# Recurrent attention and a squared-ReLU layer on one core: asking for the next pair's inputs a few product rows later, with the opening and the first groups put in another order

## The chip, the core and the metric

The kernel runs on one NeuronCore of a Trainium2 chip. The metric is the device time of one execution in microseconds (us), as the median of several runs. Besides the timed runs there is one profiled execution, from which every row and line below comes. The engines are called as in the profile: PE (TensorE's matrix products), PEld (its weight loads), DVE (VectorE), ACT (ScalarE), POOL (GpSimd) and SP (SyncE, which here only issues transfers).

## What is computed

```python
# attention: B=4 batches, H=8 heads, S=768 steps, D=48 per head
for t in range(S):
    state = alpha[:, :, t, :, None] * state + einsum('bhd,bhe->bhde', k[:, :, t], v[:, :, t])
    y[:, :, t] = einsum('bhd,bhde->bhe', q[:, :, t], state)
x = y.transpose(0, 2, 1, 3).reshape(B * S, H * D)      # 3072 tokens x 384
# feed-forward layer
h = maximum(x @ w_in, 0.0)                             # 384 -> 2048
out = (h * h) @ w_out                                  # 2048 -> 384
```

All of q, k, v and alpha arrive in 32-bit floats. The two weight matrices arrive in 64-bit floats.

## The kernel before

**Blocks, pairs and groups.** The sequence is cut into chunks of 128 steps, which gives 24 blocks (six chunks by four batches). Attention treats blocks two at a time, called a pair here. Four blocks make a group of 512 tokens, and the feed-forward layer runs once for each of the six groups, numbered 0 to 5. While the layer of one group runs on PE, attention for the next group's blocks is woven into it.

**One block of attention.** `load` (L119) brings alpha, q, k and v, each 192 KB, in a transfer of their own. `ln` (L258, ACT) takes the logarithm of alpha, `cs` (L280, and L283/L284 for later blocks, PE) sums it up along the steps, `eb` and `ei` (L291, L295, ACT) make the factor and its inverse, `mq` and `mk` (L299, DVE) scale q and k by them. `kT`/`qT` (L351) and later `turn` (L567) transpose on PE, and `kc`/`qc` (L365, later L575) copy the result out of PSUM. `sc` (L410) and `kv` (L438) form scores and state sums on PE, `am` (L421), `us` (L451) and `st` (L467, L468) mask and advance the state on DVE. `ga` and `gb` hold these for the two blocks of the pair `n0` and also the products y (L390) of the pair before; `ev` (L605, ACT or DVE) copies y into x, the layer's input.

**The layer.** In group 0 it uses plain 32-bit products: `ffn_in` (L908) with its relu and square on ACT (L914, L917). Later groups split each operand into parts (`b`, `l`, `d` of weights and `a`, `l`, `d` of activations) and use three fast products instead: L715 for the first matrix, L798 for the second. The parts of the weights are made once during groups 0 and 1 (`prepare`: L647 on ACT, then L642 twice on DVE), stored to DRAM by L652, and fetched again by L683 when a buffer is free.

**The weights' conversion.** A piece of 64-bit weights is loaded by L136 or L140 and turned into 32 bits in three steps, `convert_first` (L163, L167 on DVE), `convert_middle` (L177, L180 on ACT) and `convert_second` (L188, L192, L195 on DVE).

**What sets the order.** Each engine executes its own instructions in the order in which the Python code emits them. Three devices set that order.

- The opening is written out by hand, as a string of steps (`AT['first']`), and `AT['pre']` gives its first loads. In that string `ha0` is the first half of hidden tile 0 (the 256 tokens of blocks 0 and 1) and `hb1` the second half of tile 1; `zeros` is a set of three products on zeros whose result nobody reads.
- After it, `weave` goes through a list of units of PE work, each with a cost in product rows (a row is about six L715 products), and emits every event whose time, in rows, has come.
- `attention` makes the events of a pair from two tables of times (`PLAN`, `EARLY`) and numbers of `AT`: `g0`, `g1` and `g` say when each pair starts in group 0, group 1 and the groups after, `sc0` stretches the table in group 0, `ga` and `gb` are the rows at which those two stand.

In `attention`, the loads of the next pair's inputs are events too. They hang on the step that frees their buffer: alpha on `cs`, q on `turn`, keys on `ga` and `gb`, v on `gb`:

```python
        def loads(at, *which):
            out.extend((at, load, (m, x)) for m, x in which if m < NBLK)
```

SP issues all transfers in the order of emission: the inputs, the stores of parts (L652), their fetches (L683), a small row of factors through DRAM (`bl`, L317, and `br`, L327) and the outputs (L922). At most eight transfers are in flight, as transfer i waits for transfer i-8 to land. An issue that waits holds up everything behind it on SP.

## Time and profile before

| | |
|---|---|
| timed runs | 525.36, 529.82 and 524.78 us; median 525.36 us |
| the profiled execution | 526.78 us, of which its span is 525.0 us |
| PE busy | 511.3 us, 97% of the span |
| DVE busy | 362.9 us, 69% |
| ACT busy | 305.2 us, 58% |
| transfers | 102.35 MB, mean 195 GB/s |
| granted TensorE clock | 1.00 in every slice |

The page divides the span into 40 slices of 13.1 us and gives the busy share of each engine. A matmul's end is modelled, so a busy PE only says that matmuls followed each other without a hole. Its waits (who waited for whom) tell what ended each hole; "issue" there means that the engine waited for nothing that the profile shows.

### The profile page before, as it was taken

The numbers are of one execution on the slowest core, as the hardware profiler recorded it, in microseconds if no ns is written. First come the engines' busy times: TensorE is split into PE (matmuls) and PEld (weight loads), VectorE is DVE, ScalarE is ACT, GpSimd is POOL, SyncE is SP. The second block draws the span as 40 slices with busy tenths as digits, with TensorE's granted clock in tenths as the row PEclk, the third lists the DMA queues.
The fourth block names the chain that finished last, engine by engine and source line by source line (L and its number), as shares of the span: only waits on it lengthen the run. The fifth ranks groups of instructions, "written<-read, shape, count | busy, mean of one in ns | idle before, by whom it ended". The sixth has DMA issues, their size and how long they took to land.

```text
span 525.0 us, 13021 instructions
## 1 busy us (share of the span) xinstructions
PE 511.3 (97%) x5346; PEld 421.9 (80%) x5346; DVE 362.9 (69%) x627; ACT 305.2 (58%) x650; POOL 5.3 (1%) x29
## 2 busy tenths in 40 slices
PE   8879999999999999999999999999999999999997
PEld 6665455669888669887899987889987899988997
DVE  3677979989879859766596566686464486463861
ACT  5658896575779645475963166953265763164620
POOL 4000000000000000000000000000000000000000
PEclk9999999999999999999999999999999999999999
DMA  9998877555589665998995787855683444699201
GB/s 189 228 248 169 238 162 180 112 153 227 182 221 218 173 192 157 286 305 201 203 263 167 236 234 196 228 162 167 208 282 126 159 151 139 212 373 308 82 2 60
DMA packets 139323, 102.35 MB, mean 195 GB/s; under 512 B 109808, under 2 KB 112896, under 8 KB 139264
## 3 DMA queue, kind: packets, MB, share of 16 engines
q1 hardware_dynamic: 139264, 101.52, 68.6%
q8 instruction: 42, 0.69, 0.5%
q14 instruction: 17, 0.14, 0.1%
HBM read 84.17 MB, written 17.33 MB: 193 GB/s over the span
## 4 chain that ended last, share of the span: by engine, by line
PE 92%; SPq 3%; issue 1%; DMA 1%; ACT 1%; DVE 1%; DVEq 0%; POOLq 0%
PE o L798 41%; PE h L715 31%; PE h L908 7%; PE y L390 4%; SPq L119 3%; PE sckv L410 2%; PE T L567 2%; PE sckv L438 2%; DMA raw<-in_moe_w_in_dram 1%; PE cs L283 1%; PE cs L284 1%; PE cs L280 1%; SPq L136 0%; ACT hid L917 0%; PE lastT L334 0%
## 5 line engine op out<-in xcount | busy, mean ns | idle before, releaser
L715 PE MATMUL h<-xa,wb 128*128 128x512 f32 x240 | 68.8, 395 | 0.0
L715 PE MATMUL h<-xl,wl 128*128 128x512 f32 x240 | 67.8, 391 | 0.9 <-issue 0.9
L715 PE MATMUL h<-xd,wd 128*128 128x512 f32 x240 | 66.7, 393 | 0.1
L605 ACT COPY x<-y 32x256 f32<-32x256 f32 (+3 forms) x134 | 47.9, 365 | 23.2 <-PE y L390 21.0
L637 DVE TENSOR_TENSOR hid<-h,hid 128x512 f32<-128x512 f32 x40 | 27.6, 689 | 46.9 <-PE h L715 46.7
L732 ACT ACTIVATE h<-h 128x512 f32<-128x512 f32 x40 | 23.3, 582 | 62.2 <-PE h L715 62.2
L798 PE MATMUL o<-wb,ha 128*128 128x384 f32 x160 | 54.4, 340 | 1.3 <-issue 1.3
L715 PEld LDWEIGHTS h<-xl,wl 128*128 128x128 f32 x240 | 45.0, 188 | 11.0 <-issue 1.1
L798 PE MATMUL o<-wd,hd 128*128 128x384 f32 x304 | 53.8, 334 | 0.0
L798 PE MATMUL o<-w_out,hid 128*128 128x384 f32 x160 | 53.7, 490 | 0.0
L798 PE MATMUL o<-wl,hl 128*128 128x384 f32 x160 | 53.5, 335 | 0.0
L798 PEld LDWEIGHTS o<-wd,hd 128*128 128x128 f32 x304 | 52.7, 188 | 0.2
L715 PEld LDWEIGHTS h<-xd,wd 128*128 128x128 f32 x240 | 44.5, 188 | 9.7 <-issue 0.5
L715 PEld LDWEIGHTS h<-xa,wb 128*128 128x128 f32 x240 | 44.3, 188 | 9.1
L798 PE MATMUL o<-wb,hx 128*128 128x384 f32 x144 | 48.7, 338 | 0.0
L798 PE MATMUL o<-wl,hx 128*128 128x384 f32 x144 | 48.1, 334 | 0.0
L908 PE MATMUL h<-x,w_in 128*128 128x512 f32 (+1 forms) x120 | 43.3, 510 | 2.9 <-issue 2.0
L798 PEld LDWEIGHTS o<-w_out,hid 128*128 128x128 f32 x160 | 29.9, 190 | 19.9 <-ACT w_out L180 0.2
L730 ACT ACTIVATE hid<-h 128x512 f32<-128x512 f32 x40 | 24.2, 606 | 29.3 <-PE h L715 29.2
L690 ACT ACTIVATE ha<-hid 128x512 fp32r<-128x512 f32 x40 | 25.4, 637 | 25.6 <-DVE hx L642 17.2
L908 PEld LDWEIGHTS h<-x,w_in 128*128 128x128 f32 x120 | 22.3, 190 | 20.4 <-issue 16.9
L642 DVE SCALAR_TENSOR_TENSOR hl<-ha,hid 128x512 fp32r<-128x512 f32 x40 | 27.5, 686 | 12.2 <-ACT ha L690 12.2
(114 smaller groups left out, 869.4 us busy)
## 6 DMA issues: line engine op xcount, KB each, us to landing
wd<-do SPq DMA_DIRECT2D x36, 384.0 KB, 4.9
wl<-lo SPq DMA_DIRECT2D x34, 384.0 KB, 4.4
wl<-li SPq DMA_DIRECT2D x32, 384.0 KB, 4.2
wd<-di SPq DMA_DIRECT2D x32, 384.0 KB, 3.5
raw<-in_moe_w_in_dram SPq DMA_DIRECT2D x8, 768.0 KB
raw<-in_moe_w_out_dram SPq DMA_DIRECT2D x8, 768.0 KB, 4.8
v_in<-in_v_dram SPq DMA_DIRECT2D x24, 192.0 KB, 4.3
out_dram<-osb SPq DMA_DIRECT2D x24, 192.0 KB, 2.4
```

Of the source, the lines that this page charges most:

```text
L119: nc.sync.dma_start(out=t[:, :, 0:D] if x in "qk" else t.rearrange("a (h d) -> a h d", h=H), in_=srcs[x][b, :, c * C : (c + 1) * C, :].rea ...
L390: ins = nc.tensor.matmul(out=ys[e][64 * half : 64 * half + D + G * e, m % 2, p // 2, t], lhsT=lhsT, rhs=rhs, start=(half, e) not in seen, ...
L410: nc.tensor.matmul(out=ps[e][HALF[h], 0, p, :], lhsT=ks[rows, p, HALF[h]], rhs=qs[rows, p, HALF[h]], start=True, stop=True, skip_group_che ...
L605: copy(out=x[kk][to : to + m, t : t + 2], in_=blk[n]["y"][e][r : r + m, :, p // 2],)
L637: nc.vector.tensor_tensor(out=o, in0=x, in1=z, op=op)
L642: nc.vector.scalar_tensor_tensor(out=o, in0=x, scalar=c, in1=y, op0=ALU.mult, op1=op)
L690: nc.scalar.activation(out=a, in_=x, func=AF.Copy, scale=NEAR * E)
L715: nc.tensor.matmul(out=acc["h", j], lhsT=here[w, "i", p][:, kk, jj * 128 : (jj + 1) * 128], rhs=x_parts[x][:, kk], start=start and kk == 0 ...
L730: nc.scalar.activation(out=hid[j], in_=x, func=AF.Copy, scale=E)
L732: nc.scalar.activation(out=x, in_=x, func=AF.Copy, scale=1.0 + E)
L798: nc.tensor.matmul(out=acc[t][:, 0:DM], lhsT=lhs[:, t * C : (t + 1) * C], rhs=rhs, start=start, stop=stop, skip_group_check=True,)
L908: nc.tensor.matmul(out=ps, lhsT=w[:, kk, c0 : c0 + 128], rhs=xT[g][kk][:, cols], start=(kk == 0), stop=(kk == KM - 1),)
```

## The change

The calls of `loads` get delays of their own, from a new tuple `later`, in product rows. It holds where the table is not stretched (`scale == 1`: groups 1 to 4), and is zero in group 0.

```diff
     def attention(t, n0, after, scale=1, begun=True, whole_at=None, turn_at=None):
         out = []
+        later = AT["later"] if scale == 1 else (0,) * 7
...
                 if f == "ga":
-                    loads(w, (n0 + 3, "k"))
+                    loads(w + later[0], (n0 + 3, "k"))
                 elif f == "gb":
-                    loads(w, (n0 + 2, "v"), (n0 + 3, "v"), (n0 + 4, "k"))
+                    for i, m, x in ((1, n0 + 2, "v"), (2, n0 + 3, "v"), (3, n0 + 4, "k")):
+                        loads(w + later[i], (m, x))
...
                 elif f == "turn":
                     out.append((w, turn, (n0,)))
-                    loads(w, (n0 + 2, "q"), (n0 + 3, "q"))
+                    loads(w + later[4], (n0 + 2, "q"))
+                    loads(w + later[5], (n0 + 3, "q"))
...
                     if f[:-1] == "cs":
-                        loads(w, (n + 2, "a"))
+                        loads(w + later[6], (n + 2, "a"))
```

The entries of `AT` that change (the others are as before):

```diff
+'later': (0, 2, 2, 0, 1, 3, 2)
-'evs': 0.65   'w_first': (44.75, 40.75, 51.5)   'w_in_at': 2.375   'w_in_by': 3.4   'room1': 22   'xs': 0.2
+'evs': 0.7    'w_first': (42.75, 40.5, 48.5)    'w_in_at': 2.5     'w_in_by': 2.6   'room1': 23   'xs': 0.0
-'g0': ((0.75, 4, False, True, 25.5), (21.25, 6, True, True), (28.25, 8, True, False))   'sc0': (2.15, 2.35, 2.35)
+'g0': ((0.5, 4, False, True, 25.5), (21.75, 6, True, True), (28.0, 8, True, False))     'sc0': (2.35, 2.35, 2.35)
-'g1': ((5.75, 8, False, 15.5), (15.25, 10, True), (34.5, 12, True))   'g': ((1.575, 6, True), (15.5, 8, True))
+'g1': ((5.5, 8, False, 16.25), (15.0, 10, True), (34.5, 12, True))    'g': ((2.075, 6, True), (14.0, 8, True))
-'g1x': 50.0   'h0': 17   'h1': 0    'evs0': 0.1   'o0': (46.5, 47.25)    'o2': (19.75, 27.0, 32.75, 34.0, 42.0, 41.75)
+'g1x': 52.5   'h0': 16   'h1': -1   'evs0': 0.5   'o0': (48.25, 47.25)   'o2': (16.75, 28.5, 30.5, 34.75, 41.25, 42.5)
-'str1': 24.5   'ga': 9.5    'gb': 12.75   'cv0': 1.125   'pre': '0a 1a 0q 0k 1k 1q'   'cp': ()
+'str1': 24.0   'ga': 10.0   'gb': 12.25   'cv0': 0.875   'pre': '0a 0q 1a 0k 1k 1q'   'cp': ('q0', 'k1', 'k0')
-'evd': (... (2, 0, 2), (2, 1, 1), (2, 1, 2), (2, 1, 3))
+'evd': (... (2, 0, 2), (2, 1, 0), (2, 1, 1), (2, 1, 2), (2, 1, 3))
-'first': '... load2k lt1 sc1 kv1 first0 load2q load3a load2v am1 ... load3v load3k ep02 kT2 weights1 kc2 zeros2 load3q
-          second0 lt0 sc2 eb3 kv2 ei3 ep03 zeros3 first1 weights2 middle1 ha0 mq3 mk3 qT3 load4k kT3 qc3 kc3 am2 load4q
-          ha1 second1 sc3 lt2 lt3 st0 kv3 am3 us2 ha2 us3 load4a first2 ya2 yb2 weights3 ep20 ep21 ha3 weights4
-          ep22 ep23 middle2 st3 hb1 load4v second2 weights5 weights6 st2 hb2 st1 hb3 hb0'
+'first': '... load2k kT1 us0 kc1 lt1 sc1 kv1 first0 load3a ... load2q load3q ei2 ya0 ln3 yb0 load3v ... weights1 load2v
+          ep02 kT2 load3k cs3 kc2 weights2 eb3 lt0 sc2 second0 ei3 zeros3 ep03 mq3 kv2 first1 middle1 ha0 qT3 mk3 load4k
+          kT3 kc3 am2 qc3 load4a ha1 second1 sc3 lt3 st0 kv3 am3 us2 lt2 us3 ha2 first2 ya2 st1 yb2 ep20 load4v ep21 ha3
+          load4q ep22 ep23 middle2 st3 weights6 second2 weights4 hb1 st2 hb2 hb0 hb3 weights5 weights3'
```

`cp` names the copies of the opening's transposes that DVE makes instead of ACT (three), `evd` those of y (one more). One of the three `zeros` sets is left out. Whichever number stands behind `weights`, the next piece in order is loaded.

More of the change, by code (lines that the diff above doesn't have):

```diff
@@ L18 @@
 GB = 4
-AT = {'evs': 0.65, 'lead': 4, 'post': 3, 'w_first': (44.75, 40.75, 51.5), 'wstep': 1.8, 'w_in_at': 2.375, 'w_in_by': 3.4, 'room1': 22, 'room': 24, 's0': 4, 'ahead': 6, 'late': 2, 'xs': 0.2, 'g0': ((0.75, 4, False, True, 25.5), (21.25, 6, True, True), (28.25, 8, True, False)), 'sc0': (2.15, 2.35, 2.35), 'g1': ((5.75, 8, False, 15.5), (15.25, 10, True), (34.5, 12, True)), 'g': ((1.575, 6, True), (15.5, 8, True)), 'g1x': 50.0, 'gx': 46.75, 'g0x': 56.25, 'k0': 2, 'h0': 17, 'k1': 4, 'h1': 0, 'h1by': 2, 'evs0': 0.1, 'tp': 'ADMD', 'tp1': 'ADAD', 'split': 8, 'o0': (46.5, 47.25), 'o1': (), 'o2': (19.75, 27.0, 32.75, 34.0, 42.0, 41.75), 'str1': 24.5, 'ga': 9.5, 'gb': 12.75, 'cv0': 1.125, 'pre': '0a 1a 0q 0k 1k 1q', 'cp': (), 'evd': ((0, 0, 0), (0, 1, 0), (0, 1, 2), (2, 0, 2), (2, 1, 1), (2, 1, 2), (2, 1, 3)), 'first': 'ln0 warm0 ln1 cs0 zeros3 ei0 mk0 eb0 mq0 kT0 cs1 qT0 kc0 eb1 load0v load2a qc0 mq1 sc0 ei1 ln2 qT1 mk1 weights0 qc1 kv0 am0 load1v us0 kT1 kc1 load2k lt1 sc1 kv1 first0 load2q load3a load2v am1 middle0 cs2 eb2 us1 ei2 ya0 yb0 mk2 ln3 mq2 qT2 qc2 cs3 ep00 ep01 load3v load3k ep02 kT2 weights1 kc2 zeros2 load3q second0 lt0 sc2 eb3 kv2 ei3 ep03 zeros3 first1 weights2 middle1 ha0 mq3 mk3 qT3 load4k kT3 qc3 kc3 am2 load4q ha1 second1 sc3 lt2 lt3 st0 kv3 am3 us2 ha2 us3 load4a first2 ya2 yb2 weights3 ep20 ep21 ha3 weights4 ep22 ep23 middle2 st3 hb1 load4v second2 weights5 weights6 st2 hb2 st1 hb3 hb0'}
@@ new lines @@
+AT = {'later': (0, 2, 2, 0, 1, 3, 2), 'evs': 0.7, 'lead': 4, 'post': 3, 'w_first': (42.75, 40.5, 48.5), 'wstep': 1.8, 'w_in_at': 2.5, 'w_in_by': 2.6, 'room1': 23, 'room': 24, 's0': 4, 'ahead': 6, 'late': 2, 'xs': 0.0, 'g0': ((0.5, 4, False, True, 25.5), (21.75, 6, True, True), (28.0, 8, True, False)), 'sc0': (2.35, 2.35, 2.35), 'g1': ((5.5, 8, False, 16.25), (15.0, 10, True), (34.5, 12, True)), 'g': ((2.075, 6, True), (14.0, 8, True)), 'g1x': 52.5, 'gx': 46.75, 'g0x': 56.25, 'k0': 2, 'h0': 16, 'k1': 4, 'h1': -1, 'h1by': 2, 'evs0': 0.5, 'tp': 'ADMD', 'tp1': 'ADAD', 'split': 8, 'o0': (48.25, 47.25), 'o1': (), 'o2': (16.75, 28.5, 30.5, 34.75, 41.25, 42.5), 'str1': 24.0, 'ga': 10.0, 'gb': 12.25, 'cv0': 0.875, 'pre': '0a 0q 1a 0k 1k 1q', 'cp': ('q0', 'k1', 'k0'), 'evd': ((0, 0, 0), (0, 1, 0), (0, 1, 2), (2, 0, 2), (2, 1, 0), (2, 1, 1), (2, 1, 2), (2, 1, 3)), 'first': 'ln0 ln1 warm0 cs0 ei0 zeros3 mk0 eb0 kT0 cs1 mq0 qT0 kc0 eb1 load0v load2a qc0 sc0 ei1 mq1 ln2 weights0 qT1 mk1 qc1 kv0 am0 load1v load2k kT1 us0 kc1 lt1 sc1 kv1 first0 load3a middle0 am1 us1 cs2 eb2 load2q load3q ei2 ya0 ln3 yb0 load3v mq2 qT2 mk2 ep00 ep01 qc2 weights1 load2v ep02 kT2 load3k cs3 kc2 weights2 eb3 lt0 sc2 second0 ei3 zeros3 ep03 mq3 kv2 first1 middle1 ha0 qT3 mk3 load4k kT3 kc3 am2 qc3 load4a ha1 second1 sc3 lt3 st0 kv3 am3 us2 lt2 us3 ha2 first2 ya2 st1 yb2 ep20 load4v ep21 ha3 load4q ep22 ep23 middle2 st3 weights6 second2 weights4 hb1 st2 hb2 hb0 hb3 weights5 weights3'}
```

## The prediction

> **What bounds the kernel.** I read the busy shares and slices first, then the chain that ended last, then who waited for whom on PE, then the timelines at the long waits.

> ```profile
> PE 511.3 (97%) x5346; PEld 421.9 (80%) x5346; DVE 362.9 (69%) x627; ACT 305.2 (58%) x650; POOL 5.3 (1%) x29
> PE   8879999999999999999999999999999999999997
> DMA  9998877555589665998995787855683444699201
> PE 92%; SPq 3%; issue 1%; DMA 1%; ACT 1%; DVE 1%; DVEq 0%; POOLq 0%
> ```

> PE is the bound: 511.3 of 525.0 us, 92% of the last chain, and only its first slices and the tail are not full. The transfers are nearly saturated only in the first 40 us. An order of events can save only what PE loses in holes: 525.0 - 511.3 = 13.7 us, less the tail of 3.5 us and the first loads. PE's waits, longest first:

> ```profile
> PE h L908 <- issue: 2.0, 1, 2.0
> PE y L390 <- issue: 1.7, 3, 0.7
> PE o L798 <- issue: 1.3, 1, 1.3
> PE h L715 <- issue: 0.9, 1, 0.9
> PE h L908 <- ACT x L605: 0.8, 1, 0.8
> PE sckv L438 <- DMA v_in<-in_v_dram: 0.5, 1, 0.5
> ```

> (Columns: us in total, times, the longest.) The waits for another engine or a transfer all lie in the opening. The largest have no partner: "issue". In PE's compiled program (a plain 32-bit product is four instructions, a fast one or a transposition two, a wait one) these holes stand at instructions 450, 1218, 5570, 7362, 8130 and 9155: always whole multiples of 256 apart, to one. The DMA queue for instructions shows what that is, a quiet stretch ahead of two holes and then one packet (end of one view, then of the other):

> ```profile
> q8 instruction: 1, 0.02, 2.3%
> ...
> q8 instruction: 1, 0.02, 2.6%
> ```

> The first is from 35.5 to 38.3 us, the second from 238.5 to 241.3 us; 30.5 to 35.5 and 235.2 to 238.5 us show none. Over the span the queue has 42 packets for 0.69 MB. So PE's program comes in packets of about 16 KB, 256 instructions, and PE stands still when the next isn't there. Comparing the packets' landings with the instruction that PE was at, a packet is asked for about 300 instructions ahead, queues behind the transfers in flight (0.1 to 8.5 us) and is usable some 1.4 us after its arrival. A stretch of 256 quick instructions (4 to 6 us, small attention products) gives it too little time.

> The opening's large hole and what it delays, PE then ACT:

> ```profile
> 34.84 1.35 PE L908 MATMUL h<-x,w_in 128*128 128x256 f32 x5
> 38.23 1.24 PE L908 MATMUL h<-x,w_in 128*128 128x256 f32 x5 [2.04 <-issue]
> 40.30 7.16 PE L908 MATMUL h<-x,w_in 128*128 128x256 f32 x26 [0.84 <-ACT x L605]
> ...
> 38.64 0.38 ACT L914 ACTIVATE r<-h 128x256 f32<-128x256 f32 x1 [1.76 <-PE h L908]
> 39.49 0.75 ACT L605 COPY x<-y 32x256 f32<-32x256 f32 x2
> ```

> The last product of `ha3` is the first one after the boundary and waits 2.04 us. ACT's relu (L914) and square of `ha3` come ahead of the last two copies of x (L605), so x ends at 40.24 us and `hb1` waits for it until 40.30.

> **The change, part by part.**

> *The opening's order.* One `zeros` set, three plain products of 12 instructions in all, is gone, and steps change places. By the compiled order the boundary at 1218 now falls on the fifth product of `hb1`; `ha3` is at 1197 to 1208. So neither `ha3`, its relu nor the copies of x are held by the packet. Against it, v of block 2 is asked for behind v of 3, and `kv2` waits for it about 0.37 us longer. The packet for the boundary is asked for some 0.35 us later than before (30.9 for 30.5 us), so I put it usable at 38.6 us. Work behind it can start there and not at 40.30: -1.7 us. The bounds: nothing (the packet comes 1.7 us later still, as behind the transfers of one more weight piece) and -2.1 us (x ends at 38.2). The missing `zeros` products cost nothing: they (six passes of about 0.22 us) stand where PE waits for v of block 2 anyway; without that wait they would be a gain of 1.3 us.

> *The loads later.* They stand in groups 1 to 4 only. A row is six products of 0.227 us (144 L715 products take 32.68 us), 1.36 us, so a load goes back by 1.4 to 4.1 us. From issue to first use, before: the tightest alpha pair (blocks 10, 11) lands at 145.1 and is used at 150.7 us, 5.6 us; k of 11 has 5.1 us (its own delay is 0), k of 17 7.4, v of 10 10.8, alpha of 16 10.5, q of 10 11.9, the rest at least 14. Alpha of 10 goes back 2.7 us, and behind one more store of parts on SP, leaving about 2. No wait is left on PE: cost 0. If this cover were gone, a pair's alpha 2 us late would hold PE for up to 2 us a pair. On SP the stores, fetches and outputs that stood behind these loads now go first; they get no later. [...]

> *The groups' events.* They move the boundaries in time, and so the holes. I compared PE's nominal time for the 256 instructions before each boundary in both programs, and the margin of before (negative: a hole). At instruction 4034 it goes from 5.85 to 4.61 us (margin 1.5 to 0.26); at 5570 4.99 to 4.33, less one load that no longer goes ahead of the packet (the hole stays at 0.95); at 6338 6.02 to 4.72 (2.0 to 0.7); at 7362 4.32 to 5.41 (a hole of 0.7 goes); at 7618 6.07 to 4.76 (a hole of 1.3 appears); at 8130 3.16 to 4.08 (1.27 to 0.35); at 9154 4.95 to 6.10 (0.37 goes). The sum of the holes is 3.15 us before and 2.55 after: -0.6 us. The bounds: all gone, -3.15; every one as at 1218, 2.04 us at seven boundaries, +11.1.

> *Group 0's end.* The second part of piece 6 of w_out now stands behind that of piece 7 on DVE, whose work there fills 11.7 to 11.9 of every 12.5 us. Its part is ready at 118.1 us by DVE's nominal time, and PE needs it at 118.07 to 118.25. I take +0.3 us, bounds 0 and +1. In group 1 weight parts come ahead of `mk` and `mq` by one DVE operation of 0.95 us; the thinnest margin of transposed q and k was 0.14 to 0.6 us, in the second pair. Bounds 0 and +0.8; I take 0, as that pair's start moves earlier too (15.25 to 15.0 rows). The further copies on DVE in the opening lie beside PE's wait for loads.

> **Sum.** -1.7 + 0.3 - 0.6 = -2.0 us against the profiled execution: 526.78 - 2.0 = 524.8 us. That execution is 1.42 us above the median of the runs; the median should follow: 525.36 - 2.0 = 523.4 us.

> **The rivals.**

> *A. The opening's hole only moves.* The packet comes when the transfers in flight let it, and the reordered loads put `load4v` and two weight pieces closer to it. Then the hole, 2 us, stays on the path and the rest balances: 525.4 us. For it: a hole of 2.04 us at the same boundary, in a stretch with transfers at 9 tenths. Against it: x no longer depends on it. [...]

> *B. Slower: the later loads stand in front of PE's packets.* In groups 1 to 4 the loads now leave near the small products whose stretch of 256 is shortest. A load of 192 KB takes 1.1 us to land behind another (0.9 to 1.2 us between landings in the opening). With one more ahead of each of the seven packets, the margins above give holes of 0.84, 2.05, 0.4, 0.93, 2.4, 1.45 and 0.53, sum 8.6 us: 6.05 more, 529.5 us. With two it is 16.3 us and 537 us. I put it at 531. It decides from 0.3 us of delay a packet on, the first margins. For it: the packet at 241 us waited about 3 us behind fetches and loads. Against it: the same packets have such company before, and spread loads can also clear the way.

> *C. All packets come in time.* Holes after the opening vanish (-3.15), the opening gives -2.1, group 0 nothing: 525.36 - 5.25 = 520.1 us, 520.0 rounded down. For it: four of the seven stretches get longer or lose a load. Against it: 7618 and 4034 get shorter.

> *D. The delays do nothing.* It is contained in the sum, at zero.

> **How the numbers follow.** Forecast 0.40, A 0.12, B 0.24, C 0.24. One per cent, 5.25 us, is about what a measurement of this kernel tells from no change. Faster by over that needs 520.1 or less: most of C, 0.19, and 0.03 of the forecast's edge, 0.22. Slower needs 530.6: 0.21 of B and 0.03 from delays of a thin pair, 0.24. The rest, 0.54, is within. The range goes from 517.5, C with the `zeros` gain of 1.3 and 1.2 us of PE elsewhere, to 531.5, just over B; the forecast's own range is 521.5 to 525.5.

> **What would show it.** Right: no hole over 1 us at `ha3`, x copied by 38.3 us and `hb1` going by 38.7; no wait of PE for `a_in`, `q_in` or `v_in` after 45 us; holes called "issue" at 5570 and 7618, none at 7362. Wrong: PE waiting for DVE or ACT in groups 0 to 3, for loads in groups 1 to 4, or "issue" holes above 5 us together.

## The result, and the profile after

The changed kernel takes 524.86 us, the kernel before 526.92 us, as medians of 20 runs each; the ratio is 0.9962 (95% interval 0.9944 to 0.9981), 1.0 to 3.0 us less. Three runs of the kernel before, of 847 to 1300 us, are left out of the ratio, and its median without them is 525.97 us. The forecast was 2.0 us less, a median of 523.4 us, and within 1%. The profiled execution of after took 524.59 us, its span 522.8 us against 525.0 us.

The page of after, busy time, slices and chain as shown of before:

```profile
PE 511.1 (98%) x5340; PEld 421.1 (81%) x5340; DVE 365.5 (70%) x632; ACT 304.1 (58%) x645; POOL 5.3 (1%) x29
PE   8799999999999999999999999999999999999997
PE 92%; DVE 2%; ACT 2%; SPq 1%; DMA 1%; issue 1%; POOLq 0%; DVEq 0%
```

PE is still the bound, its slices full from the third to the tail, and does six passes less, the set of zeros (a pass is one matmul of the profile; a plain 32-bit product is two). The lines of its waits in after that matter here (us in total, times, the longest):

```profile
PE sckv L410 <- ACT ks L365: 1.7, 1, 1.7
PE sckv L410 <- DVE ks L365: 0.8, 1, 0.8
PE h L908 <- DVE x L605: 0.8, 1, 0.8
PE sckv L410 <- DVE qs L365: 0.8, 1, 0.8
PE h L715 <- ACT x L605: 0.8, 2, 0.4
PE h L715 <- issue: 0.5, 1, 0.5
PE y L390 <- issue: 0.2, 1, 0.2
```

The holes called issue are down from 5.9 to 0.7 us. The opening's hole of 2.0 us and those at 318, 345 and 399 us are gone; at 241 us 0.5 is left of 0.9. In their place stand waits for copies of q and k in the opening, and two of 0.4 us for copies of x, at 248 and 329 us, within the layers of groups 2 and 3. The end of the opening, PE and then ACT of after:

```profile
34.51 1.50 PE L390 MATMUL y<-am,v_in 64*48 64x64 f32 x64
35.94 2.07 PE L908 MATMUL h<-x,w_in 128*128 128x256 f32 x8
38.80 7.94 PE L908 MATMUL h<-x,w_in 128*128 128x256 f32 x28 [0.80 <-DVE x L605]
```

```profile
37.81 0.38 ACT L914 ACTIVATE r<-h 128x256 f32<-128x256 f32 x1
38.78 0.75 ACT L605 COPY x<-y 32x256 f32<-32x256 f32 x2
```

Hidden tile 0's last product isn't held any more, and `hb1` goes on at 38.80 instead of 40.30 us. But there are two passes more to do from there (28 for 26), and the last products y, at 33.41 us before, came 1.1 us later.

For a comparison at equal work I gave every product its mean duration by kind from the profile of before, holes left out, and cut each trace where 449.5, 300, 270, 200 and 100 us of such work were left. Each row is one profiled execution, in us, up to the start of PE's last product; the kernels below the second row are the experiments.

| kernel | opening, to 449.5 left | 449.5 to 300 | 300 to 270 (holds 241 us) | 270 to 200 | 200 to 100 (holds 318, 345, 399 us) | rest |
|---|---|---|---|---|---|---|
| before | 60.17 | 153.50 | 32.30 | 70.77 | 105.86 | 98.54 |
| after | 59.46 | 153.58 | 31.95 | 71.83 | 103.69 | 98.45 |
| later_only | 58.95 | 154.38 | 32.01 | 70.77 | 107.92 | 98.54 |
| opening_only | 60.87 | 153.55 | 32.32 | 70.77 | 108.01 | 98.54 |
| no_later | 60.68 | 153.55 | 32.50 | 71.88 | 103.69 | 98.45 |
| groups_only | 58.52 | 154.10 | 34.47 | 71.55 | 103.69 | 98.44 |
| after_z12 | 61.08 | 153.67 | 32.51 | 71.38 | 103.69 | 98.44 |
| groups_nz | 58.25 | 153.56 | 31.09 | 72.11 | 103.69 | 98.44 |
| before_p96 | 61.93 | 153.54 | 34.01 | 72.31 | 102.83 | 98.54 |
| before_p48 | 63.59 | 153.56 | 35.93 | 75.50 | 102.83 | 98.54 |

Between before and after: opening -0.7, the stretch with 241 us -0.35, the next +1.1 (the first of the two waits for x, at 249 us, and a hole of 0.2 at 265 us), the stretch with 318, 345 and 399 us -2.2. Together -2.2 us.

The openings of the table can't be compared as they stand, for the granted clock differs. The profiles of opening_only and no_later show it at 0.50 for 3.4 us, from 24.8 and from 23.6 us on, while PE works without a pause. In windows of 2 us of opening_only (the clock stands behind the number of matmuls):

```profile
24.00:26.00 2.00, 2.00 (x37) 0.71 0.66 139
26.00:28.00 2.00, 2.00 (x35) 0.50 1.12 351
```

Half of that time, 1.6 to 1.7 us, is lost, so I put both openings at about 59.2 us at full clock, an estimate. After has such a stretch from 16.1 to 19.5 us, ahead of a wait of 1.7 us that takes it up; groups_nz has one from 15.8 to 19.2 us, ahead of a wait of 1.2 us; before, later_only, groups_only and after_z12 have none in the opening.

### The profile page after: what moved, and what is told of

Same layout as the page of the kernel before. It is cut to its first block, busy times and chain, and to the rows that moved or that the text cites. A ratio compares the mean times of both kernels' runs of the same rounds, so it can differ in the third digit from the quotient of the medians.

```text
span 522.8 us, 13015 instructions
## 1 busy us (share of the span) xinstructions
PE 511.1 (98%) x5340; PEld 421.1 (81%) x5340; DVE 365.5 (70%) x632; ACT 304.1 (58%) x645; POOL 5.3 (1%) x29
## 4 chain that ended last, share of the span: by engine, by line
PE 92%; DVE 2%; ACT 2%; SPq 1%; DMA 1%; issue 1%; POOLq 0%; DVEq 0%
PE o L798 40%; PE h L715 30%; PE h L908 8%; PE y L390 5%; PE sckv L410 2%; PE T L567 2%; PE sckv L438 2%; ACT x L605 1%; SPq L119 1%; DMA v_in<-in_v_dram 1%; PE cs L280 1%; DVE x L605 1%; DVE osb L637 0%; PE cs L283 0%; PE cs L284 0%
## 5 line engine op out<-in xcount | busy, mean ns | idle before, releaser
L715 PE MATMUL h<-xd,wd 128*128 128x512 f32 x240 | 68.5, 398 | 0.8 <-issue 0.5
L715 PE MATMUL h<-xa,wb 128*128 128x512 f32 x240 | 68.5, 394 | 0.8 <-ACT x L605 0.8
L715 PE MATMUL h<-xl,wl 128*128 128x512 f32 x240 | 67.7, 390 | 0.0
L605 ACT COPY x<-y 64x256 f32<-64x256 f32 (+3 forms) x132 | 47.0, 365 | 26.9 <-PE y L390 20.5
L798 PE MATMUL o<-wb,ha 128*128 128x384 f32 x160 | 54.4, 340 | 0.0
L798 PE MATMUL o<-w_out,hid 128*128 128x384 f32 x160 | 53.7, 490 | 0.0
L798 PE MATMUL o<-wd,hd 128*128 128x384 f32 x304 | 53.7, 334 | 0.0
L798 PE MATMUL o<-wl,hl 128*128 128x384 f32 x160 | 53.6, 335 | 0.0
L715 PEld LDWEIGHTS h<-xa,wb 128*128 128x128 f32 x240 | 44.5, 188 | 10.7 <-ACT x L605 1.7
L715 PEld LDWEIGHTS h<-xl,wl 128*128 128x128 f32 x240 | 45.1, 188 | 9.7
L798 PEld LDWEIGHTS o<-wd,hd 128*128 128x128 f32 x304 | 52.8, 188 | 0.0
L715 PEld LDWEIGHTS h<-xd,wd 128*128 128x128 f32 x240 | 43.9, 188 | 10.6 <-issue 1.6
L798 PE MATMUL o<-wb,hx 128*128 128x384 f32 x144 | 48.4, 336 | 0.0
L798 PE MATMUL o<-wl,hx 128*128 128x384 f32 x144 | 48.2, 334 | 0.0
L798 PEld LDWEIGHTS o<-w_out,hid 128*128 128x128 f32 x160 | 29.9, 190 | 19.7
L908 PE MATMUL h<-x,w_in 128*128 128x512 f32 (+1 forms) x120 | 43.7, 514 | 0.9 <-DVE x L605 0.8
L908 PEld LDWEIGHTS h<-x,w_in 128*128 128x128 f32 x120 | 22.1, 190 | 18.4 <-issue 14.3
L690 ACT ACTIVATE ha<-hid 128x512 fp32r<-128x512 f32 x40 | 25.4, 638 | 19.2 <-PE o L798 12.1
L637 DVE TENSOR_TENSOR osb<-o,osb 128x384 f32<-128x384 f32 x24 | 12.9, 556 | 28.2 <-PE o L798 27.0
```

The lines of the kernel that those rows point to most:

```text
L605: copy(out=x[kk][to : to + m, t : t + 2], in_=blk[n]["y"][e][r : r + m, :, p // 2],)
L637: nc.vector.tensor_tensor(out=o, in0=x, in1=z, op=op)
L690: nc.scalar.activation(out=a, in_=x, func=AF.Copy, scale=NEAR * E)
L715: nc.tensor.matmul(out=acc["h", j], lhsT=here[w, "i", p][:, kk, jj * 128 : (jj + 1) * 128], rhs=x_parts[x][:, kk], start=start and kk == 0 ...
L798: nc.tensor.matmul(out=acc[t][:, 0:DM], lhsT=lhs[:, t * C : (t + 1) * C], rhs=rhs, start=start, stop=stop, skip_group_check=True,)
L908: nc.tensor.matmul(out=ps, lhsT=w[:, kk, c0 : c0 + 128], rhs=xT[g][kk][:, cols], start=(kk == 0), stop=(kk == KM - 1),)
```

## The experiments

The theory, P: behind the opening the time hangs on where the boundaries of PE's 256-instruction packets fall, and the delays of the loads do nothing. The places bear out the first half: counting PE's passes, weight loads and waits, all 37 holes called issue in the fourteen profiles stand within one instruction of 450 plus a multiple of 256, and in before and in after the queue for instructions moves 42 packets, 0.69 MB, 16 KB each. What the holes cost is for the experiments. The first four kernels take the change apart.

**The delays alone (later_only).** The kernel before with `'later': (0, 2, 2, 0, 1, 3, 2)` and nothing else.

> The kernel before with nothing but the delays of the loads in groups 1 to 4 (`later`); PE's program is the same as before. Theory P (after the opening, the time hangs on where PE's packets of 256 instructions end, and the loads cost and bring nothing): within 0.5 us of before, with holes called issue again near 241, 318, 345 and 399 us, 2.5 to 3.5 us together. Rival L (the spread loads clear the way for the packets; the three holes missing in the profile after, at 318, 345 and 399 us, are their work): 2 to 2.5 us faster, with those holes gone. Rival B of the prediction (loads in front of packets): 4 to 6 us slower, with longer holes.

Measured: 527.17 us against 527.32, ratio 1.0005 (0.9982 to 1.0028). PE's waits of it:

```profile
PE y L390 <- issue: 2.4, 2, 2.0
PE h L908 <- issue: 1.4, 1, 1.4
PE o L798 <- DMA wd<-do: 0.9, 1, 0.9
PE o L798 <- issue: 0.4, 1, 0.4
```

The holes are at 319, 347 and 401 us again, L and B fall. None came at 241 us, where P had one too; its packet began to arrive at 237.0 us, 238.6 in before. This time the one at 319 us is 2.0 instead of 0.6 us: here the hole's place came with PE's program, which is the same in both, and its length with the execution. Behind the opening no wait for alpha, q or v is there.

**The rest without the delays (no_later).** After with

```diff
-'later': (0, 2, 2, 0, 1, 3, 2)
+'later': (0, 0, 0, 0, 0, 0, 0)
```

> The changed kernel with all delays of the loads at zero; PE's program is the same as after. Theory P: as the changed kernel, 2 us faster than before (1 to 3), no hole over 0.3 us at 318, 345 and 399 us. Rival L: the holes come back, 0 to 0.5 us faster than before.

Measured: 526.12 against 527.32, ratio 0.9968 (0.9946 to 0.9991), and no hole over 0.3 us at the three places. As P said: the whole gain is there without the delays. A wait of 1.5 us for DVE at 244 us, which after doesn't have, is in this profile.

**The opening alone (opening_only).** Before with `pre`, `cp`, `evd` and `first` of after.

> The kernel before with the opening of the changed one alone (first loads, string of steps, copies on DVE); one set of zeros less, PE's program shifted by 9 instructions from there on. Theory P: the opening gives 0.6 us, as the two profiles have it at equal work behind it; the stretches ahead of boundaries become 5.85 us at 5570 (hole gone), but 3.2 at 7362, 3.6 at 8130, 4.1 at 9154 and 2.4 in group 0, so the holes grow by 1 to 2.5 us in all: 0.5 to 2 us slower than before. Rival O (the prediction's sum: the opening gives 1.7 us, and the groups' holes stay as they were): 1.5 to 2 us faster.

Measured: 526.34 against 527.32, ratio 0.9992 (0.9965 to 1.0018). By its median ratio it is neither 1.5 to 2 us faster (O) nor 0.5 to 2 us slower (P); the interval, 1.8 us faster to 0.9 us slower, reaches into both. The table shows no gain in the opening (60.87 us, about 59.2 at full clock), a hole of 2.2 us at 320 us and one near 402, and none at 345, where P had forecast one.

**The groups alone (groups_only).** After with those four entries of before.

> The changed kernel with the opening of the kernel before. Theory P: 2.04 us of hole ahead of hidden tile 1 as before; behind it the stretches are 3.45 us at 5570, 3.4 at 8130, 4.7 at two others and over 6 at 7362 and 9154: holes of 2.5 to 3.5 us against 3.9, and 0.5 to 1 us of waits for the copies of x, new in the profile after. Within 1 us of before. Rival O (the groups give 0.3 us by the prediction's sum): 0.3 us faster, which this run can't tell from P. Rival G (the groups alone carry the measured gain, 2 us): 2 us faster.

Measured: 526.49 against 527.32, ratio 0.9988 (0.9963 to 1.0013): within 1 us of before, which P and O both said; G's 2 us, a ratio of 0.9962, lies just outside the interval. The stretch with 318 us is clean (103.69), but a hole of 2.3 us at 241 us takes 2.5 us back.

**Moved boundaries, with everything else left (before_p96, before_p48).** Small products whose result nobody reads, ahead of `hb1`, push all later boundaries back by four instructions each:

```diff
-    ... middle2 st3 hb1 ...
+    ... middle2 st3 pad24 hb1 ...        (pad12 in the second kernel)
+    for _ in range(k):   # k = 24 or 12
+        nc.tensor.matmul(out=ps[0:64, 0, 0:64], lhsT=ident[0:48, 0:64], rhs=ident[0:48, 0:64], start=True, stop=True)
```

> The kernel before with 24 small products (48x64 on 48x64, result never read) ahead of the second half of hidden tile 1, in PE's wait of 0.6 to 0.8 us for x: every later boundary falls 96 instructions earlier in the work. Nominal cost 48 passes of 0.022 us, 1.04 us, of which 0.8 hidden. Theory P: the shortest stretches ahead of boundaries are now 4.6 to 5.0 us (before: 3.2, 4.3, 4.95, 4.99), so the holes of groups 1 to 4 go from 3.2 to 3.9 us to under 1.2, and the kernel is 2 to 3 us faster than before. Rival N (the packets are late because of the transfers at those times, wherever the boundary is): holes at 241, 318, 345 and 399 us stay, 0.2 to 0.5 us slower.

> The same with 12 such products, 48 instructions, nominal cost 0.52 us, all of it hidden in the wait for x. Theory P: the stretches ahead of the boundaries near 243 and 266 us are 2.1 us, the shortest there can be (a whole stretch of small attention products), all others over 6; two holes of 2 to 3 us each, none near 318, 345 and 399 us: 1 to 2.5 us slower than before, and 3.5 to 5 us slower than with 96. Rival N: as before within 0.5 us, and no slower than with 96.

Measured: 531.41 us with 96 instructions and 530.50 us with 48, against 526.38; ratios 1.0096 (1.0067 to 1.0125) and 1.0085 (1.0057 to 1.0113). P's totals are wrong for both. Three things were mis-sized or left out. The small products, one behind the other, take not 0.022 but 0.063 us a pass:

```profile
38.26 3.01 PE L962 MATMUL pad<-ident 48*64 48x64 f32 x48
```

The openings are 1.8 us (96) and 3.4 us (48) longer than in before's own row, but not by the padding alone, which is half as long with 48. With 96 the granted clock is 0.50 from 14.7 to 21.6 us, and the products y, ahead of the padding, already come at 34.66 us for 33.41; with 48 it is 0.50 from 38.8 to 45.6 us. Second, the two holes that P forecast with 48 did come, 1.8 us at 243 and 3.1 us at 273, but each is followed by another 3.4 us at half clock. Third, though the holes at 318, 345 and 399 us went with both, as P said and N denied (102.83 us in that stretch, the best of all rows), a long stretch didn't help at 241 and 267 us. When a packet is asked for is not recorded; that it is about 300 instructions ahead of its boundary is an estimate, from the profiles of before and after, where the earliest packets begin to arrive 297 and 299 instructions ahead. By it the packet for 241 us was asked for at 232.7 us with 96, some 6.5 us before PE came to the boundary; it had landed by 239.8. The end of the DMA view from 232 to 238.3 us, then that from 238.3 to 240 us:

```profile
q1 hardware_dynamic: 2531, 1.57, 90.1%
```

```profile
q8 instruction: 1, 0.02, 5.4%
```

Three fetches of 384 KB and two loads of q are issued in the first window, and not one packet of instructions is in it. So in this stretch the packet seems to come when the burst ends, wherever the boundary falls. That is theory P2: a hole takes a boundary, and either a stretch too short for its packet or transfers that keep the packet back. N is wrong on the place; on the transfers this view fits it.

**The two openings with the same boundaries (opening_p104, nz_p108).** Two more padded kernels, to be compared with the one with 96: before with the opening of after and 26 such products, and before without `zeros2` and with 27.

> The kernel before with the opening of the changed one and 26 small products (104 instructions, less the 9 that this opening has fewer: 95), so that the groups' boundaries lie as with 96 in the kernel before. What differs from that kernel is the opening alone. Theory P: the missing hole ahead of hidden tile 1 (0.6 to 2.0 us in three profiles of that opening) is made up by the second pair's scores coming 1.1 to 1.6 us later: equal to the kernel with 96 within 0.7 us. Rival O: 1.7 us faster than it.

> The kernel before without the set of zeros that the change drops, its opening else unchanged, and with 27 small products (108 instructions less 12: 96), so the groups' boundaries lie as with 96. The boundary that held hidden tile 0's last product falls into the small products behind it. Theory P: the relu and the copies of x are no longer late, and the scores of block 2 no longer stand behind 1.4 us of zeros: 0.5 to 2 us faster than the kernel with 96, 3 to 4.5 us faster than before. Rival H (the wait for x or for the packet is only met one step later): equal to it within 0.5 us.

Measured: ratios 1.0105 (1.0064 to 1.0145) and 1.0096 (1.0060 to 1.0132), about the same as with 96. Neither O's 1.7 us for the new opening nor P's 0.5 to 2 us for the second shows, but with six runs of each kernel the comparison leaves about 2.5 us either way, so none of the forecasts is excluded. The padding itself, 3 us long, also delays `hb1` here, so these two say little on the unpadded kernel.

**The set of zeros put back (after_z12).** After with

```diff
-    ... eb3 lt0 sc2 second0 ...
+    ... eb3 lt0 zeros2 sc2 second0 ...
```

> The changed kernel with the dropped set of zeros put back ahead of the scores of block 2, where PE waits 1.7 to 2.0 us for the copy of k: its six passes (1.3 to 1.5 us) lie in that wait and cost nothing there. Every later boundary falls 12 instructions earlier in the work. Theory P2 (a packet that is late holds PE if the stretch ahead of its boundary is short or the transfers in flight hold it up): the stretches at 241 us go from 4.3 to 3.0 us and at 345 us from 4.1 to 3.0, so a hole of 1.5 to 2 at 241 and one of 0.5 to 1 at 345: 1 to 2.5 us slower than the changed kernel, 0 to 1 us slower than before. Rival O (only the opening's order and PE's work matter): as the changed kernel, 2 us faster than before, or slower by the 1.5 us of the zeros if they don't hide.

Measured: 528.00 against 526.98, ratio 1.0025 (0.9999 to 1.0051): some 3 us slower than after by the two ratios, a little beyond P2's 1 to 2.5 us. Twelve instructions put the opening's hole back on `ha3`:

```profile
34.70 1.50 PE L390 MATMUL y<-am,v_in 64*48 64x64 f32 x64
36.13 1.13 PE L908 MATMUL h<-x,w_in 128*128 128x256 f32 x4
38.91 1.46 PE L908 MATMUL h<-x,w_in 128*128 128x256 f32 x6 [1.65 <-issue]
41.20 5.01 PE L908 MATMUL h<-x,w_in 128*128 128x256 f32 x21 [0.84 <-ACT x L605]
```

and made one of 1.6 us at 242 us, as P2 said; the forecast hole at 345 us did not come. In this one profile the opening is 1.6 us longer than in after. Rival O's second branch, unhidden zeros, would show about as much there, and the times alone don't tell the two apart. The rows do: the last products y come at 34.70 us, 0.2 us later than in after, so the zeros are nearly hidden, and `hb1` goes on at 41.20 us, 2.4 us later, behind the hole.

**Small products taken apart (spread_a, spread_b).** After with the pair's small products in four runs instead of two, so that no stretch is short: the scores and sums of the first block, y, the rest of y, and the second block are events of their own 1.5 rows apart.

```diff
-    out.append((w, ga, given))
+    out.append((w, ga_sums, (n0,)))
+    out.append((w + 1.5, ga, (*given, False)))
...
-    out.append((w, gb, given))
+    out.append((w, gb, (old, None)))
+    out.append((w + 1.5, gb, (None, n0)))
```

> The changed kernel with each pair's small products in groups 1 to 4 taken apart: the scores and sums of the first block at row 10.0, the products y of the pair before at 11.5 and 13.0, the second block at 14.5 (after: 10.0 and 12.25). The same products on PE. Theory P2: the stretches ahead of boundaries are 5.3 us and more but for 4.1 at 241 us and 4.7 at 345: holes of 0.4 to 1 us against 1.1 in the profile after, 0.5 to 1 us faster than the changed kernel, 2.5 to 3 us faster than before. Rival X (the copies of x come 0.75 rows later, and the next group waits for them): the two waits of 0.4 us for x become 1.4 us each, 1 to 2 us slower than the changed kernel.

> The same taken apart 0.5 rows earlier (9.5, 11.0, 12.5, 14.0): stretches of 5.2 us at 241 and 4.3 at 345, others from 5.8 up. Theory P2: 0.5 to 1.3 us faster than the changed kernel, 2.5 to 3.3 faster than before. Rival X: the waits for x become 0.7 us each, about as the changed kernel.

Measured: ratios 1.0287 (1.0248 to 1.0327) and 1.0083 (1.0053 to 1.0114), 15 and 4 us slower than before. P2's forecast is wrong. In spread_a, the one with the later rows, PE waits elsewhere:

```profile
PE sckv L410 <- ACT inv L295: 4.9, 4, 2.0
PE h L718 <- issue: 1.5, 1, 1.5
```

Spread_b has no hole called issue behind the opening, but takes 464.8 us from 449.5 us of work on, against 459.5 in after. Group 1 alone takes 91.5 us, 87.6 in after. Two new waits for DVE (0.8 us each) are in it, and every further change from the layer's products to small ones and back costs about 0.3 us: 0.34 and 0.15 us from one start to the next, where 0.17 and 0.015 us are usual within a run. The rest is not assigned. So removing holes by taking the products apart cost more here than the holes. The edit also puts the loads that stand behind `gb` 1.5 rows later, so these two don't test the length of the stretches alone. X named the wrong wait.

**The groups with the old opening, without the zeros (groups_nz).** After with `pre`, `cp`, `evd` and `first` of before, less `zeros2`.

> The changed kernel with the opening of the kernel before, but without the set of zeros ahead of the scores of block 2: its boundaries after the opening lie within 3 instructions of the changed kernel's, and the one at 1218 falls on the fifth product of the second half of hidden tile 1, as there. What differs from the changed kernel is the order of the opening alone. Theory P2 (what the change gives comes from where the boundaries fall; its new opening order costs 0.5 to 1.5 us, as the second pair's scores come later): 2.5 to 3.5 us faster than before, 0.5 to 1.5 us faster than the changed kernel. Rival O (the new order of the opening is what brings the gain): no faster than the changed kernel with its groups alone, 0 to 1 us faster than before. Rival E (the two orders of the opening are worth the same): 2 us faster than before.

Measured: 524.08 us against 527.85, ratio 0.9935 (0.9909 to 0.9961): 3.4 us faster than before (2.1 to 4.8), as P2 said; O falls. It is the fastest kernel of the study. Its interval still overlaps with that of after, so E isn't excluded by the times; in runs at full clock the two take 523.9 us (4 runs) and 524.3 us (8 runs). PE and its waits:

```profile
34.65 2.40 PE L908 MATMUL h<-x,w_in 128*128 128x256 f32 x8
37.39 0.70 PE L908 MATMUL h<-x,w_in 128*128 128x256 f32 x2 [0.35 <-DVE x L605]
38.38 7.16 PE L908 MATMUL h<-x,w_in 128*128 128x256 f32 x26 [0.29 <-ACT x L605]
```

```profile
PE sckv L410 <- ACT ks L365: 1.4, 2, 1.2
PE h L715 <- ACT x L605: 0.8, 2, 0.4
PE y L390 <- issue: 0.4, 1, 0.4
```

The same 26 passes are left at 38.38 us as in before at 40.30.

## Why the prediction was right or wrong

The time, its direction and the range were right. The sum was right by two errors that cancel, so the closeness of the total is luck.

- *The opening, -1.7 us.* The mechanism held: no hole at `ha3`, `hb1` on at 38.80 where the text had 38.7 us, and the zeros put back bring the hole back. (The last copies of x, though, end at 39.5 us and not by 38.3.) The term was wrong. At equal work it is -0.7 us between the two profiles, and no gain over three profiles of each order: 60.17, 58.95 and 58.52 us before, 59.46, 60.68 and 60.87 after, means 59.2 and 60.3, or 59.2 for both with the two stretches at half clock taken out. Two steps failed. The hole of before was taken at the 2.04 us of one execution, where others have 1.4 and 0.6. And of the new order only v of block 2 was counted as later, by 0.37 us, a wait that after doesn't show; the scores of block 2 wait for the copy of k until 23.99 us (22.40 before), and y comes 1.1 us later. The kernel that keeps the old order and drops the zeros shows what leaving them out, with the boundary that this moves, is worth by itself: 58.25 us in one profile, about 1 us under the mean of the old order.
- *The missing zeros, nothing.* Nearly right: put back, they lie in the wait ahead of the scores of block 2 (1.7 us in after) and y comes 0.2 us later. That wait is for the copy of k, not for v as the text had it. Their twelve instructions mattered more than their 1.4 us: they move every later boundary.
- *Group 0's end, +0.3 us.* From 449.5 to 300 us left, 153.58 against 153.50 us: nothing, within its bounds.
- *The loads, nothing.* Right, and shown: alone 1.0005; without them the gain stays.
- *The holes of the groups, -0.6 us.* Right in place for four of seven (none at 4034, 7362 and 9154, a smaller one at 5570; none came at 7618 and 8130, and one of 0.2 us came at 6338), but the size was -2.2 us in the stretch with three of them, and -4.2 against later_only, which runs the same PE program and has 3.4 us at half clock there. The step that failed is the delay of the packets: I carried each over from before. The new hole of 1.3 us at instruction 7618 did not come, as its packet, asked for at 318.3 us by the estimate of 300 instructions ahead, arrived after 2.5 us; before it was asked for at 316.9 and took 5.8 us. So the same boundary had two delays. The text also read the transfers as nearly saturated in the first 40 us only; the DMA row that it shows has nine tenths again in the slices from 210 to 236 and from 249 to 276 us, on both sides of the hole at 241.
- *Waits for copies of x in groups 2 and 3, +0.8 us.* Not in the sum, and by the text's own list PE waiting for ACT there is a sign of being wrong. They come with the groups' events (in `groups_only`, `no_later`, `after_z12` and `groups_nz` too) and not with the opening.

Of the rivals, A was nearest for the opening, which brings no gain, though not by a hole that moves. B's delays of packets happen, but putting the loads later neither brings them nor takes them away in the times. C was right for three holes of the four.

What is shown is that the delays do nothing, and that the gain comes with the groups' events and the missing zeros together. That the three holes at 318, 345 and 399 us hang on the places of the boundaries is shown too: the padded kernels keep before's groups, move the boundaries, and lose all three. after_z12 moves them by twelve instructions whose work is nearly hidden, and loses 3 us. How long a hole gets is not foretold by any of the theories, and how the total splits between holes and the stretches at half clock that follow some of them was not tried apart.

## What to carry to other kernels

Look first at holes that have no partner, and at where they stand in the engine's program: here a removed or added instruction ahead shifted all the later ones (twelve in after_z12 brought holes of 1.65 and 1.6 us), so a small edit is measured together with a shift it did not mean. Before crediting an order of events, compare the kernels at equal work, stretch by stretch, in several executions, and with the granted clock of each stretch beside it; one profile gave here 2.0 us for a hole that is between 0.6 and 2.0. The fix that pulled products apart was paid for here, with 15 and 4 us, in waits for other engines and in more changes between kinds of products.

## What the runs showed of the hardware that was not expected

*A hole can cost more than its length.* PE's timeline of the kernel with the delays alone, and its granted clock (the column behind the number of matmuls) in windows of 2 us:

```profile
318.79 0.57 PE L390 MATMUL y<-am,v_in 64*48 64x64 f32 x23 [1.99 <-issue]
320.09 1.23 PE L715 MATMUL h<-xl,wl 128*128 128x512 f32 x3
321.12 1.49 PE L715 MATMUL h<-xd,wd 128*128 128x512 f32 x3
...
324.42 0.86 PE L715 MATMUL h<-xd,wd 128*128 128x512 f32 x3
```

```profile
320.00:322.00 2.00, 2.00 (x8) 0.59 0.45 177
322.00:324.00 2.00, 2.00 (x7) 0.55 0.00 0
```

The same stretches explain much of the spread between runs, for each run's mean granted clock is on record. Of the 81 runs of before that the experiments' ratios compare, 31 have a mean clock of 0.999 or 1.000 and take 525.7 us on average; 27 at 0.996 or 0.997, which 3.4 us at half clock make of it, take 527.4 us; the 23 below take 528.3 us. At 0.999 and more, after takes 524.3 us (8 runs), 1.4 us less than before: part of the measured gain may be fewer such stretches.

*Small products alone are slow.* A row of 48x64 passes took 0.69 us for 32 among the attention's products (0.022 us each), and 3.01 us for 48 (0.063 us each) when all had the same operands and wrote the same place. Which of the two made the difference wasn't tried.

*An instruction packet seems to wait for a burst to end.* In eleven profiles the packet for about 241 us was asked for at 231.7 to 237.0 us, by the estimate of 300 instructions ahead. In eight of them it began to arrive between 238.2 and 238.8 us, in the others at 236.8, 237.0 and 239.6. That it waits for the burst is read from these times; no run took the burst away. The two early ones are in kernels with the delays (groups_nz, later_only), but so is the latest (after_z12), so what the delays do to this one packet stays open.
